# A gated mix of long convolution and attention: the convolution's tail added by GpSimd instead of TensorE, the short convolution on the whole array, 84 tiles of exponentials on VectorE

## The chip, the cores and the metric

One core of one Trainium2 chip. The metric is device time in microseconds for one execution. A core has five engines with a queue each: TensorE (PE, its weight loads are listed as PEld), VectorE (DVE), ScalarE (ACT), GpSimd (POOL) and SyncE (SP, which only issues transfers here). Each engine works its queue off in order and waits on semaphores that other engines raise.

## The reference

Sequence length S = 2048, width D = 640, 32 heads of width 20, one key and value head for all of them.

```
x = A_q;  g = sigmoid((x * gate_w).sum(-1))
a: k_shift = sum over 4 taps of A_k shifted by t, times A_shift_k     # short convolution
   kv = k_shift * A_v
   y  = causal convolution of kv with A_ssm_k, 2048 long, per channel  # by FFT in the reference
   a  = x * (y + kv * A_ssm_D)
b: q = x wq;  k = x wk;  v = x wv
   p = softmax(q k^T * 20 ** -0.5)          # 32 heads x 2048 x 2048
   b = (p v) wo
out = g * a + (1 - g) * b
```

## The kernel before, in words

**Attention.** The work is cut into 32 steps G (a block I of 512 queries, and a group of four heads that lie on four strips of 32 partitions) of 16 key blocks j. A tile is one (G, j): four strips of 128 x 512 scores. TensorE makes scores with the array split by rows (score, L1473), ScalarE takes the exponential of three or two strips at a time out of PSUM (EXP, L1510, into ETA of 1536 columns and ETB of 1024 in turn), and TensorE multiplies by the values with the array split into four strips of columns (PVmm, L1552) into PSUM bank 6. The tiles that DVE_J lists for a step go past ScalarE: their scores are made between the others (the "dqk" groups), VectorE turns them into int16 numbers (L1536, once for each strip) and makes the exponential from the bits in four passes over 2048 columns (L1545), and TensorE multiplies each of the four results by values with other weights (vneg). DVE_J holds 83 tiles.

**Normalising.** Each step ends with a copy of bank 6 by VectorE (acc, L1630), a reciprocal, a trip through memory (rbc) and a product on GpSimd (oTn or oT, L1647).

**The convolutions.** The short one (kshift, L1813 and the lines above it) is a product with diagonal matrices: for each of 5 groups of 128 channels and 4 blocks of tokens, 16 products of 128 x 128 x 128, each issued by mm4 (L822 to L825) as four matmuls on strips of 32 columns. The long one goes by transforms in two blocks of 1024: for each group c of 128 channels and each of 4 groups fc of frequencies (20 units in all) spectra (L1858) makes the spectra X of kv and K of the convolution's weights on TensorE, mac (L1910) multiplies them on GpSimd in 14 instructions (6 products Pp, 2 sums Pp, 4 sums Y, 2 sums AB), and inverse (L1932) transforms back. The second block of outputs needs X0 K1 + X1 K0 and the part of X0 K0 that runs past the first block, its tail. In the frequency domain that tail is X0 K0 turned by a quarter with a sign that alternates with fc. The kernel before folds it into K1: in spectra 16 more products of 128 columns for each unit add the turned K0 to K1's place in PSUM (8 for the real, 8 for the imaginary part), and a third plane of ssm_kT holds the negative of the first, which VectorE makes five times (kneg, L1836).

**The order of the work.** Nothing of it is written by hand. The program builds a graph of operations and a list scheduler (Scheduler) runs through it with costs, latencies and constants at the top of the file; the order on each engine is what it finds. Scores, exponentials and value products have an order of their own; everything else fills in by priority. SLACK0 says by how much a filling matmul may delay the next main one, MODE which way of splitting the array a group uses (a change of it costs SWITCH), PATIENCE, EAGER, HURRY1 and HURRY2 when VectorE's scores go in by themselves, IDLE, WAITP and HOLD when GpSimd may start beside VectorE. spectra is paced: unit u waits for the exponential at a share of 0.12 to 0.85 of them all (L1865, and the lines on soft), so the 20 units are spread evenly. If TensorE has had little to do, the scheduler puts in matmuls with zeros (L2033).

Of the kernel before, what the change touches and what calls it, by code (L numbers as in the profile page):

```python
# [7 lines left out]
ALU = mybir.AluOpType  # L8
AX = mybir.AxisListType

BF16 = dt.bfloat16
# [14 lines left out]
SLA = 0.4  # L26
SLB = 0.3
SLACK = 0.05
SLACK0 = 0.3
FILL = 0.6  # L30
FWIN = 3.4
FGAP = 0.1

MODE = {"qk": "r", "dqk": "r", "pv": "c", "fillc": "c", "q2": "m", "kc": "c", "spec": "c", "inv": "c", "op": "c", "op1": "c",
        "qpc": "c"}
SWITCH = 0.096
PATIENCE = 2.0
ROOM = 0.3
OLD = 1.0
YOUNG = 6.0  # L40
WAITN = 0.5
EAGER = 99.0
AHEAD = -1.0
HOLD = 0.05
EVP = 0.0
NPRO = 400
IDLE = 0.6
WAITP = 4.0
PVB = 2
NET = 3  # L50
NE = 5
# [133 lines left out]
class Scheduler:  # L185
# [425 lines left out]
    def emit(self, nc):  # L611
# [66 lines left out]
        for cm in reversed(cms):  # L678
# [6 lines left out]
NF = 8  # L685
NG = 4
CW = 128
# [8 lines left out]

SIDE = (7, 5)
DBK = (5, 7)
HUNGER = -5.0
PORTP = 0.05  # L700
PORTD = 0.14
PORTW = 0.1
# [11 lines left out]
REJOIN = 18  # L714
TABV = (2.2e-3, 1.05e-3)
STAGES = ((0, 256, 6), (256, 128, 5), (384, 128, 6))
DVE_J = ((), (), (3, 7, 11), (3, 5, 11, 14), (2, 8, 9), (6, 12), (2, 8, 13), (6, 9, 12),
# [4 lines left out]
SCALE = float(DH) ** -0.5  # L722
CK = SCALE * LOG2E * 128.0
OCT = math.log(2.0) / 128.0
# [38 lines left out]
C4X = 0.63  # L763
# [6 lines left out]
def c_mm(n):  # L770
    return 0.005 + 0.417e-3 * n


class Kernel:
# [67 lines left out]
    def alloc(self):  # L842
        nc = self.nc
        T = self.T
# [64 lines left out]
        spec = []  # L909
# [1 line left out]
            spec += [(f"X{i}", [128, 2, 2, 2, CW], BF16), (f"K{i}", [128, 2, 2, 2, CW], BF16)]  # L911
        spec += [("Pp", [128, 3, 2, 2, CW], F32), ("Y", [128, 2, 2, 2, CW], F32)]
        spec += [(f"EX{i}", [128, 512], F32) for i in range(NEX)]
        spec += [("ssm_kT", [128, 3, NF, CW], BF16)]
        last = [("wo", [128, NDC, D], BF16), ("oTp0", [128, NDC, 512], BF16), ("oTp1", [128, NDC, 512], BF16)]
        region("R2", early0, early, spec + late, last)
        def over(name, under, off, shape, dtype):
# [862 lines left out]
    def kshift(self):  # L1780


        T = self.T
        k, v = self.aps["A_k"][0], self.aps["A_v"][0].rearrange("(b p r) d -> p b r d", p=128, r=4)
        self.dma(T["wtap"][:, :, :], self.aps["A_shift_k"].rearrange("(c p) j -> p c j", p=128), writes=["wtap"],
                 nbytes=5120, prio=3, after=self.crow0, lat=3.0)
        self.dve(lambda e: e.memset(T["kTr"][:, :, 12:16], 0.0), (), [("kTr", -1)], 0.2, prio=20, after=self.crow0)
        w = self.g.writer
        early = [w["qT0", 1, 4]]
        for b in range(NB):  # L1790
            late = self.crow0 + (early if b > 2 else [])
            o, i = T["kTr"][:, :, 16 + 512 * b:528 + 512 * b], k[512 * b:512 * b + 512, :]
            x = self.g.add("sp", lambda e, o=o, i=i: e.dma_start_transpose(o, i), (), [("kTr", b)], 0.1, kind="d",
                           nbytes=655360, prio=14 + b, lat=1.6, after=late, name="ld_k")
            x.iss = 3.3
            self.dma(T["kv"][:, 4 * b:4 * b + 4, :], v[:, b, :, :], writes=[("kvl", b)], nbytes=655360,
                     prio=14.5 + b, name="ld_v", after=late)
        sh = [128, NDC * 4, 128]
        self.dve(lambda e: e.tensor_tensor(
            T["kdiag"][:, :, :, :].rearrange("p c j d -> p (c j) d"), T["ident"][:, :].unsqueeze(1).to_broadcast(sh),  # L1800
            T["wtap"][:, :, :].rearrange("p c j -> p (c j)").unsqueeze(2).to_broadcast(sh), ALU.mult),
            ["ident", "wtap"], ["kdiag"], c_ps(2560), prio=16, port=True, name="ksh", after=[self.g.writer["kT4", NB - 1, 0], self.wq_cp])
        for c in range(NDC):
            for q in range(NB):
                pr = 24.0 + 4.0 * c + 0.5 * q
                gr = self.group("kc", pr)
                for ii in range(4):
                    for j in range(4):
                        t0 = 16 + 512 * q + ii - j
                        self.mm(gr, lambda e, bk, ii=ii, j=j, t0=t0, c=c: self.mm4(e, self.bank(bk, 128, 128 * ii), T["kTr"][:, c, t0:t0 + 509:4], T["kdiag"][:, c, j, :],  # L1810
                            start=(j == 0), stop=(j == 3)), [("kTr", q), ("kTr", q - 1), "kdiag"], c_mm(128))
                kvp = T["kv"][:, 4 * q:4 * q + 4, 128 * c:128 * c + 128]
                self.evac(gr, "dve", lambda e, bk, kvp=kvp: e.tensor_tensor(  # L1813
                    kvp, self.bank(bk).rearrange("p (i d) -> p i d", i=4), kvp, ALU.mult), [("kvl", q)],
                    [("kv", c, 4 * q + x) for x in range(4)], c_dve(512))
# [13 lines left out]
    def ssm_kT(self, c, base):  # L1829

        T = self.T
        for blk in range(2):
            src = self.scr_k[c][1024 * blk:1024 * blk + 1024].rearrange("(b p r) d -> p b (r d)", p=128, r=4)
            self.dma(T["ssm_kT"][:, blk, :, :].rearrange("p (b r) d -> p b (r d)", r=4), src, reads=[("scr_k", c)],
                     writes=[("ssm_kT", blk)], nbytes=262144, prio=base - 100, name="ld_ssmk")
        self.dve(lambda e: e.tensor_scalar(T["ssm_kT"][:, 2, :, :], T["ssm_kT"][:, 0, :, :], -1.0, None, ALU.mult), [("ssm_kT", 0)],  # L1836
                 [("ssm_kT", 2)], C4X, port=True, prio=base - 100, name="kneg")

    def conv(self):
        T = self.T  # L1840
# [17 lines left out]
    def spectra(self, c, fc, base):  # L1858

        T = self.T  # L1860
# [2 lines left out]
        kt = T["ssm_kT"]  # L1863
        f0 = 128 * fc
        pace = self.exps[int(len(self.exps) * (PACE0 + (PACE1 - PACE0) * u / (NG * D // CW)))]  # L1865
        first = 2 if fc % 2 else 0
        for kind in ("X", "K"):
            Z, z = T[f"{kind}{p}"], (kind, p)
            ex = self.nex % NEX
# [6 lines left out]
            for par in range(2):  # L1876
# [6 lines left out]
                for comp, mc in order:  # L1883
                    n = 2 * mc + par
                    lhs, tk = self.table("TO" if par else "TE", comp, mc, f0)
                    rhs, rk = rhs_of(n)
                    if kind == "K" and (comp, mc) == (0, NG - 1):
                        if par == 0:
                            l0, t0 = self.table("TE", 0, 0, f0)
                            self.mm(gr, lambda e, bk, l0=l0: self.mm4(e, self.bank(bk, 128, 0), l0, T["Drow"][:, c % 2, :], start=False, stop=False),  # L1890
                                [t0, ("Drow", c % 2)], c_mm(128))
                        for cf in range(2):
                            pl = first if cf else 2 - first
                            for mf in range(NG):
                                l1, t1 = self.table("TO" if par else "TE", cf, mf, f0)
                                self.mm(gr, lambda e, bk, l1=l1, cf=cf, pl=pl, n=2 * mf + par: self.mm4(e, self.bank(bk, 128, 128 + 256 * (1 - cf)), l1, kt[:, pl, n, :], start=False, stop=False),
                                    [t1, ("ssm_kT", pl)], c_mm(128))
                    self.mm(gr, lambda e, bk, lhs=lhs, rhs=rhs, comp=comp, st=(comp, mc) == (0, 0), sp=(comp, mc) == (1, NG - 1): self.mm4(e, self.bank(bk, 256, 256 * comp), lhs, rhs, start=st, stop=sp), [tk] + rk, c_mm(256))
                gr.mms[0].soft = {pace} - gr.mms[0].deps
                gr.mms[0].deps |= gr.mms[0].soft  # L1900
# [9 lines left out]
    def mac(self, c, fc, p, prio):  # L1910

        T = self.T
        P, Y, W, z = T["Pp"], T["Y"], T["AB"], u_of(c, fc)

        def tt(out, a, b, alu, reads, writes, n, cost=None):
            f = lambda e: e.tensor_tensor(out, a, b, alu)  # L1916
            self.pool(f, reads, writes, cost or c_pool(n), prio=prio, port=True, name="mac")

        sh = [128, 2, 2, CW]
        for h in range(2):  # L1920
            X, K = T[f"X{p}"][:, h], T[f"K{p}"][:, h]
# [171 lines left out]
```

## Time and profile before

| | us |
|---|---|
| median of 3 runs | 820.15 (818.24 to 820.39) |
| the profiled execution's own time | 812.48 |
| its span from first to last instruction | 810.7 |

| engine | busy, us | share of the span | instructions |
|---|---|---|---|
| PE | 770.7 | 95% | 13513 |
| PEld | 317.9 | 39% | 13517 |
| DVE | 663.1 | 82% | 1102 |
| ACT | 790.6 | 98% | 706 |
| POOL | 380.4 | 47% | 370 |

The profile is of one execution. Busy time counts the stretches in which at least one instruction of an engine runs; instructions overlap, so the mean of one times the count can be more than the busy time. TensorE's four strips run side by side, and the ends of its matmuls are modelled.

### The profile page before, as it was taken

How to read it: one execution, taken by the hardware profiler on the slowest of the kernel's cores; microseconds unless marked ns; L12 is line 12 of the kernel's file. 1: busy time of each engine (PE TensorE's matmuls, PEld its weight loads, DVE VectorE, ACT ScalarE, POOL GpSimd, SP SyncE). 2: the span in 40 equal slices, each digit the busy share in tenths (PEclk: the TensorE clock that was granted, in tenths of full speed). 3: DMA queues.
4: the chain of work that ended last, by engine and by line, in shares of the span. 5: the costliest groups of instructions: out<-in, count | busy, mean ns of one | idle time of the engine just before them, and what ended most of it. 6: DMA issues, size and time to landing. Idle time of an engine off the chain costs nothing.

```text
span 810.7 us, 29855 instructions
## 1 busy us (share of the span) xinstructions
PE 770.7 (95%) x13513; PEld 317.9 (39%) x13517; DVE 663.1 (82%) x1102; ACT 790.6 (98%) x706; POOL 380.4 (47%) x370
## 2 busy tenths in 40 slices
PE   8999999999999999999999999999999999999997
PEld 5244432344323443433433433443333433243344
DVE  7757899898888788899788888888899977947954
ACT  7999999999999899999999999999999999999996
POOL 4340000058766636577445677467666664600000
PEclk9999999999999999999999999999999999999999
DMA  8889111200112000011002120001000000041111
GB/s 229 196 172 194 35 49 47 57 10 23 48 49 54 23 10 21 24 48 42 16 23 56 46 65 23 16 23 36 21 23 23 17 15 15 4 120 64 56 57 35
DMA packets 65743, 42.26 MB, mean 52 GB/s; under 512 B 43379, under 2 KB 60496, under 8 KB 65616
## 3 DMA queue, kind: packets, MB, share of 16 engines
q1 hardware_dynamic: 65040, 40.14, 18.9%
q8 instruction: 105, 1.72, 0.9%
q10 hardware_dynamic: 576, 0.22, 0.1%
q14 instruction: 22, 0.18, 0.1%
HBM read 22.93 MB, written 11.13 MB: 42 GB/s over the span
## 4 chain that ended last, share of the span: by engine, by line
ACT 61%; PE 34%; DVE 4%; issue 1%; DMA 0%; DVEq 0%
ACT ETA L1510 37%; ACT ETB L1510 24%; PE ps L1473 12%; PE ps L824 10%; PE ps L1552 9%; DVE ES L1536 1%; PE ps L2033 1%; PE ps L1199 0%; DVE ES L1545 0%; DMA xn<-in_A_q_dram 0%; PE ps L1085 0%; PE ps L1713 0%; PE ps L1380 0%; DVE X L1905 0%; DVE EX L1902 0%
## 5 line engine op out<-in xcount | busy, mean ns | idle before, releaser
L1510 ACT ACTIVATE ETA<-ps 128x1536 bf16<-128x1536 f32 x344 | 524.4, 1525 | 8.6 <-PE ps L1473 5.3
L1510 ACT ACTIVATE ETB<-ps 128x1024 bf16<-128x1024 f32 x343 | 379.6, 1107 | 0.0
L1473 PE MATMUL ps<-qT,kT 32*128 32x512 bf16 (+2 forms) x2176 | 331.8, 371 | 27.4 <-ACT ETA L1510 13.1
L1536 DVE TENSOR_SCALAR ES<-ps 128x512 int16<-128x512 f32 x332 | 221.7, 686 | 69.9 <-PE ps L1473 66.5
L1545 DVE TENSOR_SCALAR ES<-ES 128x2048 int16<-128x2048 int16 x332 | 236.8, 768 | 4.7 <-PE ps L1552 2.5
L1473 PEld LDWEIGHTS ps<-qT,kT 32*128 32x128 bf16 x2176 | 84.5, 91 | 264.2 <-ACT ETB L1510 94.4
L1916 POOL TENSOR_TENSOR Pp<-X,K 128x512 f32<-128x512 bf16 x120 | 144.0, 1211 | 68.7 <-DVE ES L1545 37.2
L1552 PE MATMUL ps<-ETA,vaug 128*32 128x512 bf16 (+2 forms) x1106 | 134.4, 369 | 0.8 <-issue 0.8
L1552 PE MATMUL ps<-ETB,vaug 128*32 128x512 bf16 (+2 forms) x738 | 133.1, 369 | 0.0
L1552 PE MATMUL ps<-ES,vneg 128*32 128x512 bf16 x1328 | 117.6, 383 | 0.0
L1647 POOL TENSOR_TENSOR oTn<-acc,rbc 128x512 bf16<-128x512 f32 x24 | 36.3, 1513 | 123.0 <-DVE ES L1545 122.5
L1916 POOL TENSOR_TENSOR Y<-Pp 128x256 f32<-128x256 f32 x80 | 59.4, 742 | 38.1 <-DVE ES L1545 30.8
L1916 POOL TENSOR_TENSOR Pp<-Pp 128x512 f32<-128x512 f32 x40 | 51.6, 1291 | 38.3 <-DVE ES L1545 29.3
L1916 POOL TENSOR_TENSOR AB<-Y 128x512 bf16<-128x512 f32 x40 | 51.7, 1302 | 26.3 <-DVE ES L1545 22.0
L1552 PEld LDWEIGHTS ps<-ES,vneg 128*32 128x32 bf16 x1328 | 33.4, 95 | 40.6 <-issue 18.6
L1647 POOL TENSOR_TENSOR oT<-acc,rbc 128x512 bf16<-128x512 f32 x7 | 10.1, 1437 | 74.9 <-DVE ES L1545 50.3
L1552 PEld LDWEIGHTS ps<-ETA,vaug 128*32 128x32 bf16 x1106 | 29.6, 94 | 31.9 <-issue 28.2
L824 PE MATMUL ps<-ssm_kT,TE 128*32 128x128 bf16 (+1 forms) x1280 | 40.1, 247 | 0.1
L824 PE MATMUL ps<-ssm_kT,TO 128*32 128x128 bf16 (+1 forms) x1280 | 38.3, 247 | 0.4 <-DVE ES L1536 0.4
L1552 PEld LDWEIGHTS ps<-ETB,vaug 128*32 128x32 bf16 x738 | 28.5, 94 | 22.3 <-issue 20.6
L2033 PE MATMUL ps<-TE,zeros 128*32 128x512 bf16 x352 | 30.7, 386 | 0.8 <-DVE acc L1630 0.8
L1905 DVE TENSOR_TENSOR K<-ps,EX 128x512 bf16<-128x512 f32 x40 | 27.2, 681 | 4.6 <-PE ps L824 4.3
(179 smaller groups left out, 673.7 us busy)
## 6 DMA issues: line engine op xcount, KB each, us to landing
rbc<-scr_d SPq DMA_DIRECT2D x31, 256.0 KB
scr_o<-oTn SPq DMA_DIRECT2D x24, 128.0 KB, 1.8
kv<-in_A_v_dram SPq DMA_DIRECT2D x4, 640.0 KB
scr_k<-kst SPq DMA_DIRECT2D x5, 512.0 KB
ssm_kT<-scr_k SPq DMA_DIRECT2D x10, 256.0 KB, 4.6
out_dram<-outsb SPq DMA_DIRECT2D x15, 160.0 KB
xn<-in_A_q_dram SPq DMA_DIRECT2D x3, 640.0 KB
scr_q<-xT SPq DMA_DIRECT2D x15, 128.0 KB, 1.7
```

Of the source, the lines that this page charges most:

```text
L824: x = e.matmul(out[q:q + 32], lhs[:, q:q + 32], rhs, tile_position=(0, q), **k)
L1473: return e.matmul(self.bank(bk, n, n * t), T["kT0" if first(G, jt) else "kT4"][32 * r:32 * r + 32, 128 * jt:128 * jt + 128], T[k][32 * r:3 ...
L1510: x = op("act", lambda e: e.activation(et(n)[:, 0:w], self.ps[:, lo:lo + w], ACT.Exp, scale=OCT, bias=-K0 * OCT), [("ps", base[n % 2] + k) ...
L1536: self.evac(gr, "dve", lambda e, bk, c=c: e.tensor_scalar(P[:, c], self.bank(bk), FINE, FTOP, ALU.mult, ALU.add), (), [kP[r]], c_dve(512))
L1545: V(lambda e, E=E, t=t: e.tensor_scalar(E, P, 1.0 / FINE, SHIFT[t] - FTOP / FINE, ALU.mult, ALU.add), kP, [("ES", z)], C4X, port=True, nam ...
L1552: return op("pe", lambda e: e.matmul(self.bank(b, n)[32 * r:32 * r + 32, :], v[:, j, :], src, start=(j == 0 or cut and j == 4 * EARLY), st ...
L1647: self.pool(lambda e: e.tensor_tensor(out, T["acc"][:, :], T["rbc"][:, :], ALU.mult), ["acc", "rbc"], [key], 1.27, prio=p, port=True, name ...
L1905: self.evac(gr, "dve", lambda e, bk, EX=EX, Z=Z, h=h, alu=alu: e.tensor_tensor(Z[:, h].rearrange("p i a c -> p a i c"), parts(self.bank(bk ...
L1916: f = lambda e: e.tensor_tensor(out, a, b, alu)
L2033: sch.filler, *sch.filler2 = ([[lambda e, r=r, st=st, b=b, n=n: e.matmul(self.bank(b, n)[32 * r:32 * r + 32, :], self.T["zeros"][:, 0:32], ...
```

## The change

In spectra the 16 products that add the tail go, with the third plane of ssm_kT and kneg. In mac two more GpSimd instructions for each unit add the turned first block's product to the second block's. The short convolution issues each product as one matmul on the whole array. There are two buffers EX instead of one, which takes the room of the third plane. DVE_J lists 84 tiles, at other places. Ten of the scheduler's constants change, so the whole order is made anew.

```diff
-SLACK0 = 0.3
+SLACK0 = 0.8
-MODE = {..., "q2": "m", "kc": "c", "spec": "c", ...}
+MODE = {..., "q2": "m", "spec": "c", ...}
-PATIENCE = 2.0
+PATIENCE = 1.4
-YOUNG = 6.0
+YOUNG = 2.0
-EAGER = 99.0
+EAGER = 0.8
-IDLE = 0.6
-WAITP = 4.0
+IDLE = 0.3
+WAITP = 6.0
-HURRY1 = 0.3
-HURRY2 = 0.2
-NEX = 1
+HURRY1 = 99.0
+HURRY2 = 0.0
+NEX = 2
-HUNGER = -5.0
+HUNGER = 0.0
-DVE_J = ((), (), (3, 7, 11), (3, 5, 11, 14), (2, 8, 9), ...
+DVE_J = ((), (), (5, 7, 10), (3, 7, 14), (3, 6, 10), ...
...
-        spec += [("ssm_kT", [128, 3, NF, CW], BF16)]
+        spec += [("ssm_kT", [128, 2, NF, CW], BF16)]
...
-    self.mm(gr, lambda e, bk, ...: self.mm4(e, self.bank(bk, 128, 128 * ii), T["kTr"][:, c, t0:t0 + 509:4], T["kdiag"][:, c, j, :],
+    self.mm(gr, lambda e, bk, ...: e.matmul(self.bank(bk, 128, 128 * ii), T["kTr"][:, c, t0:t0 + 509:4], T["kdiag"][:, c, j, :],
...
-        self.dve(lambda e: e.tensor_scalar(T["ssm_kT"][:, 2, :, :], T["ssm_kT"][:, 0, :, :], -1.0, None, ALU.mult), ...
...
-                        for cf in range(2):
-                            pl = first if cf else 2 - first
-                            for mf in range(NG):
-                                l1, t1 = self.table("TO" if par else "TE", cf, mf, f0)
-                                self.mm(gr, ..., l1, kt[:, pl, n, :], ...
...
+        for o, alu in ((fc % 2, ALU.add), (1 - fc % 2, ALU.subtract)):
+            tt(Y[:, :, 1, o, :], Y[:, :, 1, o, :], Y[:, :, 0, 1 - o, :], alu, [("Y", 0), ("Y", 1)], [("Y", 0), ("Y", 1)], 256)
```

## Rows read from the trace of the kernel before

**Rows 1.** The page: span, busy time and share of each engine
```profile
span 810.7 us, 29855 instructions
PE 770.7 (95%) x13513; PEld 317.9 (39%) x13517; DVE 663.1 (82%) x1102; ACT 790.6 (98%) x706; POOL 380.4 (47%) x370
```

**Rows 2.** ETA's exponentials: nanoseconds min/median/max, first and last start, forms
```profile
L1510 ACT ACTIVATE ETA<-ps x344: 628/1512/1710, 15.6 to 803.3; 128x1536 bf16<-128x1536 f32 x172
```

**Rows 3.** ACT in order of time: start, length, instruction, idle before it
```profile
61.51 1.45 ACT L1510 ACTIVATE ETA<-ps 128x1536 bf16<-128x1536 f32 x1 [2.11 <-PE ps L1473]
...
69.46 1.45 ACT L1510 ACTIVATE ETA<-ps 128x1536 bf16<-128x1536 f32 x1 [0.95 <-PE ps L1473]
...
780.45 1.56 ACT L1510 ACTIVATE ETA<-ps 128x1536 bf16<-128x1536 f32 x1
...
789.39 1.66 ACT L1510 ACTIVATE ETA<-ps 128x1536 bf16<-128x1536 f32 x1
```

**Rows 4.** Who ACT waited for: us in total, times, longest
```profile
ACT ETA L1510 <- PE ps L1473: 5.3, 9, 2.1
ACT ETA L1510 <- PE ps L824: 2.3, 1, 2.3
```

**Rows 5.** The chain that ended last, from 55 to 70 us
```profile
57.86 0.91 PE ps L824 x51
58.77 1.96 issue
...
67.19 0.79 issue
```

**Rows 6.** Stretches around the short convolution: PE, PEld, DVE, ACT, POOL, clock, DMA
```profile
47.00:58.00 11.00, 11.00 (x354) 6.50 (x355) 5.58 (x10) 10.96 (x10) 6.04 (x9) 1.00 0.72 154
58.00:70.00 12.00, 8.65 (x260) 4.61 (x248) 7.76 (x11) 8.93 (x9) 1.64 (x1) 1.00 1.05 171
70.00:116.00 46.00, 44.03 (x1118) 21.24 (x1118) 38.98 (x72) 45.60 (x42) 2.25 (x2) 1.00 0.35 72
```

**Rows 7.** Groups of instructions by shape: count, busy us, mean ns, idle before
```profile
L824 PE MATMUL ps<-ssm_kT,TO 128*32 128x128 bf16 x640 | 16.7, 220 | 0.0
L824 PE MATMUL ps<-ssm_kT,TE 128*32 128x128 bf16 x640 | 14.7, 220 | 0.0
L824 PE MATMUL ps<-kdiag,kTr 128*32 128x128 bf16 x1280 | 27.3, 222 | 2.1 <-issue 2.0
L1836 DVE TENSOR_SCALAR ssm_kT<-ssm_kT 128x1024 bf16<-128x1024 bf16 x5 | 3.6, 720 | 1.4 <-DMA ssm_kT<-scr_k 1.4
L1916 POOL TENSOR_TENSOR Y<-Pp 128x256 f32<-128x256 f32 x80 | 59.4, 742 | 38.1 <-DVE ES L1545 30.8 <-DVE ES L1536 1.6 <-DVE sq L1374 0.7
```

**Rows 8.** PE in order of time: changes of split, and transposes on the whole array
```profile
30.68 0.39 PE L1473 MATMUL ps<-qT,kT 32*128 32x512 bf16 x3 [0.20 <-ACT ETA L1510]
31.00 0.39 PE L1552 MATMUL ps<-ETB,vaug 128*32 128x512 bf16 x1
...
31.23 0.38 PE L1552 MATMUL ps<-ETB,vaug 128*32 128x512 bf16 x2
...
43.81 0.62 PE L1085 MATMUL ps<-ident,TI 128*128 128x128 bf16 x8
44.37 0.60 PE L1380 MATMUL ps<-sq,IndT 128*32 128x512 bf16 x2
```

**Rows 9.** Line L1916, GpSimd's products and sums: what ended idle time before them
```profile
  DVE ES L1545: 119.3, 55
  DVE K L1905: 26.5, 8
  DVE sq L1374: 6.9, 7
  DVE ES L1536: 6.3, 20
```

**Rows 10.** L1916's last group and VectorE's L1545: min/median/max ns, first and last start
```profile
L1916 POOL TENSOR_TENSOR AB<-Y x40: 1262/1272/1715, 186.4 to 708.3; 128x512 bf16<-128x512 f32 x40
L1545 DVE TENSOR_SCALAR ES<-ES x332: 623/687/1776, 66.1 to 773.5; 128x2048 int16<-128x2048 int16 x166
```

**Rows 11.** The stretch of the long convolution: all engines, then L1545 alone
```profile
167.00:709.00 542.00, 520.95 (x8877) 208.17 (x8870) 464.32 (x718) 538.14 (x476) 341.01 (x310) 1.00 0.10 29
...
167.00:709.00 542.00, 184.66 (x256) 1.00 0.10 29
```

**Rows 12.** VectorE's exponentials: groups by shape
```profile
L1536 DVE TENSOR_SCALAR ES<-ps 128x512 int16<-128x512 f32 x332 | 221.7, 686 | 69.9 <-PE ps L1473 66.5
L1545 DVE TENSOR_SCALAR ES<-ES 128x2048 int16<-128x2048 int16 x332 | 236.8, 768 | 4.7 <-PE ps L1552 2.5
```

**Rows 13.** The output projection and the last block's: by shape, then first and last start
```profile
L824 PE MATMUL ps<-wo,oTp 128*32 128x320 bf16 x480 | 24.5, 301 | 0.4 <-issue 0.3
...
L824 PE MATMUL ps<-wo,oTp x480: 296/299/310, 727.0 to 785.9; 128*32 128x320 bf16 x160
L1686 DVE SCALAR_TENSOR_TENSOR part<-ps,omgf,kv x8: 504/550/552, 787.7 to 805.3; 128x320 f32<-128x320 f32 x8
```

More of the change, by code (lines that the diff above doesn't have):

```diff
@@ L32 @@
 FGAP = 0.1
-MODE = {"qk": "r", "dqk": "r", "pv": "c", "fillc": "c", "q2": "m", "kc": "c", "spec": "c", "inv": "c", "op": "c", "op1": "c",
+MODE = {"qk": "r", "dqk": "r", "pv": "c", "fillc": "c", "q2": "m", "spec": "c", "inv": "c", "op": "c", "op1": "c",
         "qpc": "c"}
 SWITCH = 0.096
-PATIENCE = 2.0
+PATIENCE = 1.4
 ROOM = 0.3
 OLD = 1.0
-YOUNG = 6.0
+YOUNG = 2.0
 WAITN = 0.5
-EAGER = 99.0
+EAGER = 0.8
 AHEAD = -1.0
@@ L716 @@
 STAGES = ((0, 256, 6), (256, 128, 5), (384, 128, 6))
-DVE_J = ((), (), (3, 7, 11), (3, 5, 11, 14), (2, 8, 9), (6, 12), (2, 8, 13), (6, 9, 12),
[4 rows of a table removed]
+DVE_J = ((), (), (5, 7, 10), (3, 7, 14), (3, 6, 10), (7, 8, 13), (2, 10, 12), (6, 9, 11),
[4 rows of a table added]
 SCALE = float(DH) ** -0.5
@@ L1809, in kshift @@
                         t0 = 16 + 512 * q + ii - j
-                        self.mm(gr, lambda e, bk, ii=ii, j=j, t0=t0, c=c: self.mm4(e, self.bank(bk, 128, 128 * ii), T["kTr"][:, c, t0:t0 + 509:4], T["kdiag"][:, c, j, :],
+                        self.mm(gr, lambda e, bk, ii=ii, j=j, t0=t0, c=c: e.matmul(self.bank(bk, 128, 128 * ii), T["kTr"][:, c, t0:t0 + 509:4], T["kdiag"][:, c, j, :],
                             start=(j == 0), stop=(j == 3)), [("kTr", q), ("kTr", q - 1), "kdiag"], c_mm(128))
@@ L1835, in ssm_kT @@
                      writes=[("ssm_kT", blk)], nbytes=262144, prio=base - 100, name="ld_ssmk")
-        self.dve(lambda e: e.tensor_scalar(T["ssm_kT"][:, 2, :, :], T["ssm_kT"][:, 0, :, :], -1.0, None, ALU.mult), [("ssm_kT", 0)],
-                 [("ssm_kT", 2)], C4X, port=True, prio=base - 100, name="kneg")
     def conv(self):
@@ L1865, in spectra @@
         pace = self.exps[int(len(self.exps) * (PACE0 + (PACE1 - PACE0) * u / (NG * D // CW)))]
-        first = 2 if fc % 2 else 0
         for kind in ("X", "K"):
@@ L1891, in spectra @@
                                 [t0, ("Drow", c % 2)], c_mm(128))
-                        for cf in range(2):
-                            pl = first if cf else 2 - first
-                            for mf in range(NG):
-                                l1, t1 = self.table("TO" if par else "TE", cf, mf, f0)
-                                self.mm(gr, lambda e, bk, l1=l1, cf=cf, pl=pl, n=2 * mf + par: self.mm4(e, self.bank(bk, 128, 128 + 256 * (1 - cf)), l1, kt[:, pl, n, :], start=False, stop=False),
-                                    [t1, ("ssm_kT", pl)], c_mm(128))
                     self.mm(gr, lambda e, bk, lhs=lhs, rhs=rhs, comp=comp, st=(comp, mc) == (0, 0), sp=(comp, mc) == (1, NG - 1): self.mm4(e, self.bank(bk, 256, 256 * comp), lhs, rhs, start=st, stop=sp), [tk] + rk, c_mm(256))
```

8 rows, old and new, of the table DVE_J are left out of this document.

## Prediction

> **What bounds the kernel now.** I read the page first: ACT is busy 98% of the span, PE 95%, DVE 82%, POOL 47% [rows 1]. PE's figure is a poor guide, since it runs four strips side by side and much of its work is fill. So the question is whether ACT ever stops. Its exponentials start at 15.6 us and the last starts at 803.3, 787.7 us apart, 343 pairs of ETA and ETB [rows 2]. Undisturbed, four pairs take 789.39 - 780.45 = 8.94 us, 2.235 us a pair [rows 3]. 343 x 2.235 = 766.6, so ACT's row of exponentials contains about 21 us of gaps, and 15.6 us before plus 7.4 us after it belong to start and finish, which the change doesn't touch. **The kernel can get faster in two ways only: fewer columns on ACT, or fewer gaps.** It gets slower if some other engine makes new gaps, or leaves work for after the last exponential.
>
> Of the gaps the view of waits names only the long ones: 5.3 us behind scores (L1473) and 2.3 us once behind other matmuls [rows 4]. Two of the former, 2.11 and 0.95 us, lie at 61.5 and 69.5 us [rows 3], in the short convolution. There the chain that ended last is PE itself, waiting for nothing that the profile shows: 1.96 us in the middle of the short convolution's matmuls and 0.79 us a little later [rows 5]. The table by stretches says what is special: from 58 to 70 us the DMA engines are busy all the time (1.05) and PE only 8.65 of 12 us; afterwards, with the same matmuls but DMA at 0.35, PE is busy 44.03 of 46 us [rows 6]. So the stall needs a dense run of PE instructions and full DMA engines together.
>
> **The change part by part.** All sums are against the profiled execution's own 812.48 us; the three runs shown have their median at 820.15 us, 0.9% higher, so I carry the result over by ratio.
>
> *One more tile on VectorE (84 for 83).* ACT loses 4 x 512 = 2048 columns; a pair of 2560 takes 2.235 us, so ACT saves 1.79 us. VectorE gets 4 x 0.686 + 4 x 0.768 = 5.8 us [rows 12]; it stood idle 66.5 us for scores of exactly this kind [rows 12], which covers it. Without that cover the tile's values would come late and hold up the end of a step.
>
> *The tail leaves TensorE.* 1280 matmuls in two groups, 16.7 + 14.7 = 31.4 us of PE time [rows 7]. PE is not what ends last, so this counts nothing by itself; at best it thins the gaps of below a microsecond. Gaps without those three named waits: 21.1 - 2.1 - 0.9 - 2.3 = 15.8 us. I take 0 and keep both sides: half of the 15.8 us and the 2.3 us wait gone (-9), or as much again as PE fills in elsewhere under a longer SLACK0 (+5). kneg takes 3.6 us off DVE [rows 7], off the path.
>
> *The tail comes to GpSimd.* 2 instructions in each of 20 units, of the shape of Y: 40 x 0.742 = 29.7 us [rows 7], plus a wait before some of them. L1916 lost 119.3 us waiting until L1545 was done, over 280 instructions 0.43 us each [rows 9]; 40 x 0.43 = 17 us. So GpSimd needs 30 to 47 us more, in a stretch of 542 us in which it is busy 341.0 [rows 11]. I take this at nothing on the path: mac runs behind a pace set by the exponentials, and GpSimd stood waiting for its input K for 26.5 us [rows 9], nearly the bare 29.7. The other end is the first rival. AB, the last step of mac, waits for the two new sums, and inverse for AB; only the last unit's 2 x 0.74 us can't hide behind a following unit.
>
> Here a rule is to be weighed. L1545 takes 0.687 us in the median and up to 1.776 [rows 10], and it is what GpSimd waits for most [rows 9]: the two do not run together. Taken as fully exclusive, 341.0 + 184.7 = 525.7 of the 542 us are taken already [rows 11], and with 29.7 us more, 2 for the tile and 3 less of kneg it would be 554, 12 us too many. The Trainium skill, SBUF — State Buffer, section Who interferes with whom, says just this: a VectorE instruction in a two-port mode and a GpSimd instruction exclude each other for their whole length. By that rule the mac chain ends 12 us later; by the wait for K it doesn't.
>
> *The short convolution on the whole array.* 320 matmuls for 1280, and as many weight loads. On PE little changes: 27.3 us / 320 = 85 ns for four strips [rows 7], against 0.56 us / 8 = 70 ns for a whole-array product of the same size [rows 8]; 5 us of PE time, off the path. What matters is a quarter of the instructions in the stretch with full DMA engines. I take both stalls as gone, -2.11 - 0.95 = -3.06 us; the other end is 0, since the DMA load stays and the second stall came within value products. Against it: between two value products of one split 0.23 us pass, from a score to a value product 0.32 [rows 8], so a change of split costs some 0.1 us, and the short convolution now differs from both neighbours. The stretch has about 30 pairs; two changes more in each would be 6 us of PE time, against 69 - 63.7 = 5.3 us in which PE is idle there [rows 6]. The Trainium skill, TensorEngine Tiling (Array Packing), section Key Properties, has the same rule: a change of tiling mode drains the engine. By it the gain in this stretch is used up; by the pieces I expect (most lie between scores, where the split changed already) it isn't.
>
> *The second EX buffer* lets the next spectrum's evacuation start earlier: nothing on the path.
>
> **Sum:** 812.48 - 1.79 - 3.06 = 807.6 us, a ratio of 0.994; on the median 815.2 us.
>
> **The rivals.**
> 1. *GpSimd becomes the bound and the kernel is slower.* 29.7 + 17, and 2 more for the waits behind L1374 and L1536 (13.2 us over 280 instructions, times 40) [rows 9], are 49 us, less the 26.5 us of waiting for K: the last AB, now at 708.3 [rows 10], comes 22 us later. Behind it stand inverse and the output projection, 24.5 us of PE time within the 59 us from 727.0 to 785.9, and the last block's part, whose last evacuation is at 805.3 [rows 13]: there is no room behind. Each us of delay leaves 24.5 / 59 = 0.42 us of projection for after the exponentials: 9.2 us. 807.6 + 9.2 = 816.8, on the median 824.5. It decides from the point where 0.42 us times the delay exceeds the gain of 4.9: a last AB after 720 us. For it: the sum of 526 of 542 us. Against: the 26.5 us, and POOL's 59% in the stretch. With the exclusive sum alone, 12 us late, it is 807.6 + 5 = 812.7, on the median 820.5: no change.
> 2. *The gaps are only dealt anew.* The order of all engines changes; stalls of 2 to 3 us such as those at 61.5 us come up elsewhere. Only the tile is left: 810.7, on the median 818.3, no change that shows. For it: one of the three named waits has nothing to do with the short convolution. The change of split (6 us more of PE, 1 of it uncovered) ends here too.
> 3. *TensorE's relief shows.* 9 us of the other gaps go as well: 798.6, on the median 806.5. For it: 31 of 771 us of PE work go. Against: long waits for PE are few [rows 4].
> 4. *The change doesn't do what it says*: TensorE's freed time goes into matmuls with zeros. That costs nothing, and leads to rival 2.
>
> **How the numbers follow.** The bound that a measurement of this kernel can tell from no change is 0.3%, 817.7 to 822.6 us. Forecast (815.2): 0.36. Rival 1: 0.26 beyond the bound and 0.06 for its mild form by the exclusive sum. Rivals 2 and 4: 0.21. Rival 3: 0.11. Faster 0.47, same 0.27, slower 0.26. Likeliest is faster, 815.2 us, its own range 811 to 818 (both stalls gone or one, gaps 3 us fewer). The range must take in rival 1 at 824.5 with 2 or 3 us for gaps, and most of the way to rival 3: 808 to 827.
>
> **What would show it.** ACT: 2048 columns fewer, so 343 ETA or one less, and no idle time of 1 us or more between 47 and 70 us; the chain there without "issue". PE: ssm_kT with 128 columns gone, kdiag 320 times at 128*128, PE's busy time lower by some 30 us or zeros in its place. POOL: 120 Y of 256 columns, the last AB before 720 us, waiting for K below 26.5 us. The prediction is wrong in its step on GpSimd if the last AB is past 720 us and output projection runs after the last exponential; in its step on the short convolution if ACT still stops there; and in its step on gaps if span less pairs x 2.235 is still 21 us or more.

## The result and the profile after

The changed kernel takes 805.12 us in the median of four runs (804.46 to 807.77); the kernel before 819.19 (817.44 to 820.39). The ratio is 0.9836, with a 95% interval of 0.9805 to 0.9867. It is faster, then, by 1.6%, in the direction that was forecast, but by 14 us instead of 5, and below the lower end of the range.

The executions of before need a second look. The profiled one took 812.48 us, with a mean granted clock of 1.000. In the experiments' comparisons before ran some fifty times more, and no such execution came up: they lie between 816.0 and 822.9 us, with mean clocks of 0.998 to 0.987; the medians of the three sets are 819.18, 819.25 and 819.31. Those of after: 804.46 and 805.32 us at 1.000, 804.93 at 0.999, 807.77 at 0.996. The profile of before, on which every term of the sum rests, was thus its most favourable execution.

The page of after, the lines that answer to [rows 1], then the row on instruction loading and that on matmuls with zeros:

```profile
span 803.5 us, 26040 instructions
PE 759.6 (95%) x11573; PEld 304.5 (38%) x11577; DVE 663.9 (83%) x1105; ACT 788.8 (98%) x704; POOL 402.8 (50%) x410
q8 instruction: 90, 1.47, 0.8%
L2026 PE MATMUL ps<-TE,zeros 128*32 128x512 bf16 (+1 forms) x640 | 54.4, 384 | 0.4 <-DVE acc L1630 0.2
```

TensorE lost 31.4 us of tail, but its busy time fell by 11 us only. The last row shows why: matmuls with zeros take 54.4 us, where before's page has 30.7 for 352 of them. The scheduler gave 24 us of the freed time to zeros.

ACT in after: the row that answers to [rows 2], and the view of waits beside [rows 4]:

```profile
L1510 ACT ACTIVATE ETA<-ps x343: 1125/1509/1716, 15.7 to 796.7; 128x1536 bf16<-128x1536 f32 x171, 128x1024 bf16<-128x1024 f32 x1
```

```profile
ACT ETA L1510 <- PE ps L1473: 3.2, 10, 0.9
```

From the first to the last exponential 781.0 us pass; 342 pairs of 2.235 us make 764.4, which leaves 16.6 us of gaps, where before had 21.1. So the span fell by 7.2 us: 4.5 in gaps, 2.2 for one pair less (1.8 for the 2048 columns, the rest the odd piece at the end, which the tile makes longer), 0.6 in the finish, 0.1 at the start the other way. The wait of 2.3 us behind L824 is gone, and no wait of the exponentials is over 0.9 us. That accounts for the two profiles, 812.48 against 805.32. The medians differ by 14, and the other 7 us aren't in the profile of before at all.

The table by stretches [rows 6], in after; each line has the stretch and its length in us, the busy time and number of instructions of PE, PEld, DVE, ACT and POOL, the granted clock, the DMA share and GB/s:

```profile
47.00:58.00 11.00, 11.00 (x146) 6.72 (x144) 5.55 (x10) 11.00 (x10) 6.08 (x9) 1.00 0.65 144
58.00:70.00 12.00, 11.44 (x132) 5.50 (x129) 10.40 (x17) 12.00 (x12) 1.27 (x1) 1.00 1.04 175
```

From 58 to 70 us ACT works all 12 us (before 8.93), with the DMA engines as full as they were and half the PE instructions (132 for 260). The chain that ended last has no "issue" of PE there any more [rows 5]; in this stretch it goes along SP's queue:

```profile
54.97 5.16 SPq L1822
...
60.86 6.58 DMA kst<-in_A_ssm_k_dram
...
78.27 4.14 DMA den<-acc
...
82.44 0.25 DVE rcp L1640
...
85.39 1.44 ACT ETA L1510
```

A transfer for a reciprocal lands late behind the transposing loads, and ends in the one wait of 0.9 us, the longest that is left.

GpSimd: the long convolution's first product in before, then in after, then after's new sums and last group, and what its line waited for [rows 9, 10]:

```profile
L1916 POOL TENSOR_TENSOR Pp<-X,K x120: 1143/1155/1663, 167.5 to 700.4; 128x512 f32<-128x512 bf16 x120
...
L1907 POOL TENSOR_TENSOR Pp<-X,K x120: 1148/1155/1609, 152.5 to 697.9; 128x512 f32<-128x512 bf16 x120
...
L1907 POOL TENSOR_TENSOR Y<-Y x40: 723/728/736, 175.9 to 708.0; 128x256 f32<-128x256 f32 x40
L1907 POOL TENSOR_TENSOR AB<-Y x40: 1263/1272/1713, 180.0 to 713.8; 128x512 bf16<-128x512 f32 x40
...
  DVE ES L1545: 137.4, 71
  DVE K L1896: 23.1, 6
```

The sums cost 29.1 us, and the last AB starts at 713.8 us, 5.5 later than before. The first product starts at 152.5 us; before it was 167.5. The new plan gives GpSimd 15 us more room in front.

### The profile page after: what moved, and what is told of

It reads as the page before. It is cut to its first block, busy times and chain, and to the rows that moved or that the text cites. A ratio compares the mean times of both kernels' runs of the same rounds, so it can differ in the third digit from the quotient of the medians.

```text
span 803.5 us, 26040 instructions
## 1 busy us (share of the span) xinstructions
PE 759.6 (95%) x11573; PEld 304.5 (38%) x11577; DVE 663.9 (83%) x1105; ACT 788.8 (98%) x704; POOL 402.8 (50%) x410
## 4 chain that ended last, share of the span: by engine, by line
ACT 70%; PE 23%; DVE 2%; DMA 2%; SPq 2%; issue 1%
ACT ETA L1510 43%; ACT ETB L1510 28%; PE ps L1473 8%; PE ps L1552 6%; PE ps L824 5%; PE ps L2026 1%; DMA kst<-in_A_ssm_k_dram 1%; SPq L1822 1%; SPq L800 1%; DVE ES L1536 1%; PE ps L1810 1%; DMA den<-acc 1%; PE ps L1199 0%; DMA xn<-in_A_q_dram 0%; PE ps L1085 0%
## 5 line engine op out<-in xcount | busy, mean ns | idle before, releaser
L1510 ACT ACTIVATE ETA<-ps 128x1536 bf16<-128x1536 f32 (+1 forms) x343 | 521.8, 1521 | 4.3 <-PE ps L1473 3.2
L1473 PE MATMUL ps<-qT,kT 32*128 32x512 bf16 (+2 forms) x2176 | 321.0, 371 | 33.5 <-ACT ETA L1510 14.6
L1536 DVE TENSOR_SCALAR ES<-ps 128x512 int16<-128x512 f32 x336 | 222.4, 685 | 52.3 <-PE ps L1473 48.9
L1545 DVE TENSOR_SCALAR ES<-ES 128x2048 int16<-128x2048 int16 x336 | 237.9, 762 | 9.1 <-PE ps L1552 6.6
L1907 POOL TENSOR_TENSOR Pp<-X,K 128x512 f32<-128x512 bf16 x120 | 139.8, 1169 | 58.1 <-DVE ES L1545 29.0
L2026 PE MATMUL ps<-TE,zeros 128*32 128x512 bf16 (+1 forms) x640 | 54.4, 384 | 0.4 <-DVE acc L1630 0.2
L1907 POOL TENSOR_TENSOR Y<-Y 128x256 f32<-128x256 f32 x40 | 29.1, 729 | 33.2 <-DVE ES L1545 29.1
L1893 DVE COPY EX<-ps 128x512 f32<-128x512 f32 x40 | 27.2, 681 | 3.4 <-PE ps L824 3.2
L1896 DVE TENSOR_TENSOR X<-ps,EX 128x512 bf16<-128x512 f32 x40 | 27.4, 685 | 2.2 <-PE ps L824 1.6
```

Source lines behind the costliest of these rows:

```text
L1473: return e.matmul(self.bank(bk, n, n * t), T["kT0" if first(G, jt) else "kT4"][32 * r:32 * r + 32, 128 * jt:128 * jt + 128], T[k][32 * r:3 ...
L1510: x = op("act", lambda e: e.activation(et(n)[:, 0:w], self.ps[:, lo:lo + w], ACT.Exp, scale=OCT, bias=-K0 * OCT), [("ps", base[n % 2] + k) ...
L1536: self.evac(gr, "dve", lambda e, bk, c=c: e.tensor_scalar(P[:, c], self.bank(bk), FINE, FTOP, ALU.mult, ALU.add), (), [kP[r]], c_dve(512))
L1545: V(lambda e, E=E, t=t: e.tensor_scalar(E, P, 1.0 / FINE, SHIFT[t] - FTOP / FINE, ALU.mult, ALU.add), kP, [("ES", z)], C4X, port=True, nam ...
L1893: self.evac(gr, "dve", lambda e, bk, EX=EX: e.tensor_copy(EX[:, :], self.bank(bk)), (), [("EX", ex)], c_dve(512))
L1896: self.evac(gr, "dve", lambda e, bk, EX=EX, Z=Z, h=h, alu=alu: e.tensor_tensor(Z[:, h].rearrange("p i a c -> p a i c"), parts(self.bank(bk ...
```

## The experiments

In those marked *order kept* every engine has the planner's order, untouched; only the edit differs. The others are planned anew. Gaps are counted as in the prediction: from the first to the last exponential of ETA, less 2.235 us for each pair.

**Before again, unchanged (b_again).**

> The kernel before, unchanged, to see whether its 812.48 us profiled execution stands for its other executions (817 to 820 us). Theory A (stall with full DMA engines): its executions differ by the length of the stalls in the short convolution between 58 and 70 us; a profile near 818 us would show about 8 us there where the first showed 3. Rival: the difference is spread over the whole span, or lies in the start or the end; then the stretch 58 to 70 us shows the same 3 us.

Measured: 818.62 us (816.08 to 820.65), ratio 0.9994 [0.998, 1.0009]; the profile has a span of 817.9 us. Two pairs of rows show what the first profile lacked. The table by stretches in the first profile of before:

```profile
58.00:64.00 6.00, 3.43 (x126) 1.91 (x114) 2.23 (x4) 3.88 (x5) 0.00 (x0) 1.00 1.15 136
64.00:71.00 7.00, 6.08 (x173) 3.17 (x165) 5.91 (x9) 6.05 (x6) 1.64 (x1) 1.00 0.96 205
...
728.00:734.00 6.00, 5.91 (x112) 2.41 (x108) 2.96 (x6) 5.93 (x6) 0.00 (x0) 1.00 0.10 31
734.00:740.00 6.00, 6.00 (x97) 2.02 (x85) 3.48 (x6) 5.97 (x7) 0.00 (x0) 1.00 0.22 75
```

The same kernel, the same stretches, in this run:

```profile
58.00:64.00 6.00, 3.41 (x128) 1.98 (x116) 1.19 (x2) 3.62 (x4) 0.00 (x0) 1.00 1.35 147
64.00:71.00 7.00, 6.74 (x73) 1.84 (x77) 5.60 (x8) 5.13 (x5) 1.64 (x1) 0.52 0.86 190
...
728.00:734.00 6.00, 2.91 (x65) 1.32 (x57) 0.69 (x1) 2.91 (x4) 0.00 (x0) 0.95 0.36 99
734.00:740.00 6.00, 5.91 (x94) 2.22 (x86) 2.25 (x4) 4.66 (x5) 0.00 (x0) 0.77 0.02 4
```

From 58 to 64 us PE stands idle as long in both (3.43 and 3.41 us busy). Its long stall, though, is 1.96 us in the one and 2.24 in the other, where two of 0.23 and 0.24 us stand ahead of it; whether these make the difference isn't shown. The instruction after the stall, in before, in this run, and in a run further down with little to load (b_small_kst):

```profile
60.73 0.36 PE L824 MATMUL ps<-kdiag,kTr 128*32 128x128 bf16 x9 [1.96 <-issue]
...
61.77 0.36 PE L824 MATMUL ps<-kdiag,kTr 128*32 128x128 bf16 x9 [2.24 <-issue]
...
58.85 0.36 PE L824 MATMUL ps<-kdiag,kTr 128*32 128x128 bf16 x9 [0.47 <-issue]
```

After the stall the granted clock stays at 1.00 in the one and is 0.52 in the other: the level of 1.2 GHz, and only 73 instructions for 173. Near 730 us the same follows a transfer of wo that lands late, in order of time:

```profile
732.76 0.46 PE L824 MATMUL ps<-wo,oTp 128*32 128x320 bf16 x8 [3.09 <-DMA wo<-in_B_wo_dram]
...
733.69 1.45 ACT L1510 ACTIVATE ETA<-ps 128x1536 bf16<-128x1536 f32 x1 [3.09 <-PE ps L1473]
```

ACT's waits behind scores sum to 11.6 us, for 5.3 [rows 4].

```profile
L1510 ACT ACTIVATE ETA<-ps x344: 632/1514/1714, 15.8 to 810.5; 128x1536 bf16<-128x1536 f32 x172
```

The gaps are 28.1 us for 21.1, and these 7.0 us are nearly the whole difference of the spans, 817.9 - 810.7.

**The short convolution alone on the whole array, in before (b_kc_full, order kept).**

```diff
-    ... lambda e, bk, ...: self.mm4(e, self.bank(bk, 128, 128 * ii), T["kTr"]...
+    ... lambda e, bk, ...: e.matmul(self.bank(bk, 128, 128 * ii), T["kTr"]...
```

> The kernel before with the short convolution's products as one matmul on the whole array, issued in the same order as before on every engine (only the instruction's form is changed). Theory A: the stalls between 58 and 70 us go, ACT there is busy 12 of 12 us, and the time falls by 3 us at least and by up to 10 us if they are longer in most executions: 809 to 816 us. Rival 1 (the stall belongs to the full DMA engines alone): it stays, and the time is that of before, 819 us. Rival 2 (changes of split cost): slower by up to 3 us, 822 us.

Measured: 811.44 us (810.36 to 814.76), 0.9912 [0.9888, 0.9937]; its clock is 1.000 in three runs and 0.997 in one. One line of code gives 7.7 us, over half of the whole gain. The stretch, and ETA's exponentials:

```profile
58.00:70.00 12.00, 11.25 (x142) 5.95 (x141) 9.33 (x13) 12.00 (x12) 1.65 (x1) 1.00 0.98 208
...
L1510 ACT ACTIVATE ETA<-ps x344: 632/1518/1715, 15.8 to 801.0; 128x1536 bf16<-128x1536 f32 x172
```

ACT no longer stops there; the gaps are 18.6 us. Against before's good execution the span gains 2.2 us, where 3.06 were forecast: ACT works 12.00 of 12 us for 8.93, but from 70 to 116 us it is busy 44.51 us for 45.60 [rows 6], with short waits between 82 and 107 us (0.50 us the longest). Against before's usual executions it gains what follows the stall, too.

**The strips put back into after (a_kc_strips, order kept).** The same line, the other way.

> The changed kernel with the short convolution on four strips again, in the changed kernel's order. Theory A: stalls come back at 58 to 70 us and the time rises by 3 to 10 us from 805: 808 to 815 us. Rival 1: no change, 805 us; then the gain lies in the new order and in the tail.

Measured: 810.83 us (809.77 to 813.23), 0.9894 [0.9877, 0.991], 5.7 us more than after. The one execution with a clock of 1.000 took 809.77 us, so the low clock is only a part of what the strips cost here. In the profile the stall and the low clock are back:

```profile
58.00:70.00 12.00, 9.95 (x206) 4.81 (x207) 5.93 (x10) 7.44 (x7) 0.35 (x1) 0.65 1.01 184
```

**Before with strips, but with little to load (b_small_kst, order kept).** The transposing transfers of A_ssm_k, and the stores of their result, move a sixteenth; the spectra then work on other data. The first of the lines changed:

```diff
-e.dma_start_transpose(st[:, :, :], self.aps["A_ssm_k"][CW * c:CW * c + CW, :])
+e.dma_start_transpose(st[:, 0:1, :], self.aps["A_ssm_k"][CW * c:CW * c + CW, 0:128])
```

> The kernel before, strips and order unchanged, but the transposes that load the long convolution's weights move a sixteenth (and other data of the same size goes into the spectra: the output is not that of the reference). Theory A (dense PE instructions and full DMA engines together): with the DMA engines free the stalls at 58 to 70 us go although the four strips stay, granted clock 1.00 there, 809 to 813 us. Rival (dense instructions alone): the stalls stay, 817 to 820 us.

Measured: 814.32 us (811.3 to 818.42), 0.9945 [0.9921, 0.9969].

```profile
58.00:70.00 12.00, 10.68 (x322) 5.59 (x314) 9.16 (x13) 11.48 (x11) 1.66 (x1) 1.00 0.15 42
```

With the DMA share at 0.15 for 1.05 [rows 6], PE gets through 322 instructions in the 12 us, for 260, and the long stall shrinks from 1.96 us to 0.47. So the long stall needs both, many PE instructions and full DMA engines; taking away either ends it or leaves a quarter. The time is 5.0 us below before's, where 6 to 10 were expected: a late stall of 3.0 us, with the low clock behind it, remains near 728 us.

What PE waits for can be read from the trace: it is its own instructions. They come by a queue of transfers of their own, in before:

```profile
q8 instruction: 105, 1.72, 0.9%
```

That is 105 packets of 16 KB for the 13513 + 13517 instructions of PE and PEld, 257 a packet. In after 90 packets go with 11573 + 11577, again 257, and in b_kc_full 98 with 12557 + 12557, 256.

The stalls lie a packet apart. In b_again those at 51.96, 56.16 and 59.53 us come after 1217, 1473 and 1729 recorded instructions of PE and PEld, 256 from one to the next; those of a_kc_strips and b_small_kst among these products come at the same counts. In before, whose trace has four records fewer, they come after 1725 and, at 67.19 us, after 1981.

And each ends when a packet has landed. In the trace's list of transfers one goes from 58.52 to 59.48 us in before, and PE goes on at 60.73, 1.25 us after the landing. In b_again the packet lands at 60.29 and PE goes on 1.48 us later, in b_small_kst at 57.44 and 1.41 us; at the other such stalls, b_loads_free's with them, it is 1.30 to 1.75 us. In b_small_kst the packet sets out 1.9 us before PE stops, in before 0.25 us. So PE waits for its next instructions: the strips take four times as many for the same products, and beside full DMA engines the packets set out late.

**That late stall (b_loads_free, order kept).** The four transfers of a set (wo, oTp) no longer wait for each other's landing; their readers wait for the set.

```diff
+                for o in s:
+                    o.deps = base | lanes[o]
```

> The kernel before, strips and order kept, but the four loads of wo and the four of each oTp no longer wait for one another to land (they write different partitions; readers wait for all four). If the late wo load at about 733 us is the second part of what most executions of the kernel before lose, the gap of 3 us and the second episode of granted clock 0.5 there go, and the time falls from 819 to about 815 us, with the stalls at 58 to 70 us unchanged. Rival: the loads are not it, 819 us.

Measured: 816.91 us (815.12 to 818.46), 0.9974 [0.9957, 0.999]. The late stretch is whole again, but from 321 to 329 us the clock is now 0.79, where b_again has 1.00:

```profile
728.00:734.00 6.00, 6.00 (x130) 3.12 (x132) 1.38 (x2) 5.75 (x5) 0.00 (x0) 1.00 0.14 27
...
321.00:329.00 8.00, 7.45 (x115) 2.92 (x112) 4.96 (x7) 6.74 (x7) 4.99 (x5) 0.79 0.02 3
```

The gain is 2.3 us, where 4 were expected, and the short convolution (7.7 us) remains the larger cause.

**The tail taken from TensorE, nothing in its place (bk_no_tail: b_kc_full without the 1280 matmuls, order kept; the output lacks the tail).**

```diff
-self.mm(gr, lambda e, bk, l1=l1, ...: self.mm4(..., kt[:, pl, n, :], ...
+self.skip.add(self.mm(gr, lambda e, bk, l1=l1, ...: self.mm4(..., kt[:, pl, n, :], ...
```

> The kernel before with the short convolution on the whole array (b_kc_full, 811.4 us) and the tail's 1280 matmuls left out, in the same order on all engines: the output lacks the tail. It measures TensorE's relief alone. Prediction's step (off the path): 811 us within 2. Rival (31 us less for PE thins the gaps): 803 to 808 us.

Measured: 817.57 us (813.73 to 827.26), 0.9982 [0.995, 1.0013]; without the longest run the median is 816.87. That is 31 us of PE work less, and 5 to 6 us *slower* than b_kc_full; the clock was 0.977 to 0.994. The same three stretches in b_kc_full, then in bk_no_tail, there with ETA's exponentials:

```profile
316.00:324.00 8.00, 7.46 (x137) 3.08 (x137) 5.89 (x10) 8.00 (x9) 5.26 (x5) 1.00 0.02 3
324.00:340.00 16.00, 15.87 (x275) 6.53 (x271) 13.40 (x22) 16.00 (x16) 11.12 (x10) 1.00 0.09 28
...
356.00:362.00 6.00, 5.79 (x119) 2.53 (x118) 5.89 (x9) 6.00 (x7) 3.77 (x4) 1.00 0.07 22
```

```profile
316.00:324.00 8.00, 7.12 (x89) 1.92 (x77) 6.99 (x11) 8.00 (x8) 4.20 (x5) 0.91 0.00 0
324.00:340.00 16.00, 15.76 (x254) 6.42 (x252) 11.44 (x19) 15.05 (x15) 9.13 (x8) 0.94 0.09 28
...
356.00:362.00 6.00, 5.23 (x64) 1.77 (x64) 5.60 (x9) 6.00 (x6) 4.66 (x4) 0.84 0.02 7
...
L1512 ACT ACTIVATE ETA<-ps x344: 628/1532/1716, 18.4 to 805.5; 128x1536 bf16<-128x1536 f32 x172
```

Where the tail was, PE has fewer instructions (89 for 137 in the first stretch), the clock falls to 0.91 and 0.94, and ACT loses 0.95 of 16 us. In the third it falls again, to 0.84. But this profile, of an execution of 814.85 us, has 4.5 us more span than b_kc_full's, and 2.6 of them lie before the first exponential (18.4 us for 15.8), with a spell of low clock at 8 to 13 us (0.66), long before the tail's place, which begins at 152.8 us in b_kc_full; only 1.9 lie in the gaps (20.5 for 18.6). So the trace shows that the clock falls where the tail was, and ties some 1.9 us to it; the rest of the 5 to 6 between the medians isn't placed.

**The tail moved to GpSimd in the old order (bk_tail_moved: the same with the two sums before each AB, order kept).**

```diff
+        fns = [lambda e, o=o, alu=alu: e.tensor_tensor(Y[:, :, 1, o, :], Y[:, :, 1, o, :], Y[:, :, 0, 1 - o, :], alu) ...
```

> As bk_no_tail, with the two GpSimd sums of each unit put in ahead of AB, in the otherwise same order (whole computation). Prediction's step: the sums hide behind the pace, the time of bk_no_tail within 2 us. Rival 1 of the prediction: GpSimd falls behind, the last AB comes after 720 us instead of about 706, and the time is 3 to 9 us above bk_no_tail.

Measured: 828.73 us (823.68 to 831.2), 1.0111 [1.0071, 1.015], 11 us over bk_no_tail. The last group of mac in this kernel:

```profile
L1918 POOL TENSOR_TENSOR AB<-Y x40: 1263/1273/1769, 188.9 to 724.4; 128x512 bf16<-128x512 f32 x40
```

In bk_no_tail that row ends at 710.0. AB comes 14 us later (22 were forecast), and 11 to 12 us are lost (9.2 forecast), but not on the first rival's path. ETA's exponentials:

```profile
L1512 ACT ACTIVATE ETA<-ps x344: 628/1504/1715, 16.9 to 818.4; 128x1536 bf16<-128x1536 f32 x172
```

The span is 825.8 us, so 7.4 us follow the start of the last exponential, as without the sums (813.0 - 805.5 = 7.5), and no matmul of the output projection stands behind it. The loss is in the gaps, 34.9 us for 20.5: ACT waits 12.6 us behind scores for 5.3, and two spells of low clock lie between 200 and 400 us.

**After without the sums (a_no_sums, order kept; the output lacks the tail).**

```diff
-            tt(Y[:, :, 1, o, :], Y[:, :, 1, o, :], Y[:, :, 0, 1 - o, :], alu, ...
+            self.skip.add(tt(Y[:, :, 1, o, :], Y[:, :, 1, o, :], Y[:, :, 0, 1 - o, :], alu, ...
```

> The changed kernel without its 40 GpSimd sums, in its order (the output lacks the tail). If they hide, 805 us within 2; if they cost on the path, 3 to 9 us less, 796 to 802 us.

Measured: 805.09 us (804.89 to 807.67), 0.9827 [0.98, 0.9854]. In the new order the sums cost nothing that can be measured.

**After without the matmuls with zeros (a_no_zeros, order kept).**

```diff
+        self.skip = {o for o in sch.linear if o.name == "fillc"}
```

> The changed kernel without its 640 matmuls with zeros, in its order (the whole computation stays). If these zeros hold TensorE's clock, which the tail's matmuls held before, episodes of granted clock 0.5 appear in the long convolution and the time rises to 815 to 825 us. If they do not matter, 805 us within 2.

Measured: 834.21 us (830.03 to 840.95), 1.0196 [1.0134, 1.0257], with clocks of 0.928 to 0.942. The 54 us of useless work are worth 29 us, more than the 10 to 20 expected. From the page and the table by stretches:

```profile
PEclk9999999979999999997999899999879998669999
...
730.00:740.00 10.00, 7.11 (x62) 1.63 (x62) 8.23 (x15) 8.92 (x9) 3.46 (x5) 0.78 0.09 27
740.00:750.00 10.00, 9.94 (x72) 2.09 (x72) 6.98 (x11) 8.16 (x8) 4.47 (x4) 0.50 0.05 16
```

PE was busy 7.11 of 10 us; in the next 10 it is busy all along, at 1.2 GHz, for hardly more instructions.

**The tail back on TensorE in after, planned anew with one EX buffer (a_tail_pe).** The sums go; the 16 products and kneg return, as in the lines the change removed.

> The changed kernel with the tail on TensorE again (third plane, kneg, one EX buffer), its constants, its table of 84 tiles and its short convolution kept; the order is made anew. If TensorE's relief makes part of the gain, 805 plus 3 to 6 us: 808 to 811 us, and shorter if GpSimd's 40 instructions had cost anything. If the tail's place counts nothing, 805 us within 2.

Measured: 827.58 us (823.08 to 831.23), 1.01 [1.0053, 1.0147]. Slower than both. A wait of 6.0 us, behind value products, stands out in ACT's view of waits:

```profile
ACT ETB L1510 <- PE ps L1552: 6.0, 1, 6.0
```

This doesn't price the tail's place, since the order differs from 118 us on. That constants and table fit one set of operations only would agree with it; no run shows it.

**One tile back on ACT (a_83, planned anew).**

```diff
-          (10,), (2, 9, 12), ())
+          (), (2, 9, 12), ())
```

> The changed kernel with one tile fewer on VectorE (step 29 gives its only one back to ScalarE); the order up to that step is the same, behind it new. The prediction's 1.79 us for a tile: 807 us. If the tile costs VectorE or TensorE as much as it saves ScalarE: 805 us.

Measured: 817.95 us (815.56 to 823.53), 0.9989 [0.9969, 1.001]: 12.8 us more, where the columns are worth 1.8. My assumption that the order ahead of that step would stay was wrong: VectorE's and GpSimd's orders differ from some 380 us on. spectra is paced by shares of all exponentials, so another count can reach back; that this is the reason is argued, not shown. A new hole, from 580 us on:

```profile
580.00:592.00 12.00, 9.84 (x151) 3.58 (x150) 11.34 (x18) 7.35 (x8) 7.92 (x8) 1.00 0.02 3
```

**An attempt at a better version (a_better, order kept).** This goes for the wait at 85 us. Free transfers as in b_loads_free, and that reciprocal three places later:

```diff
+        r = [o for o in v if o.name == "rcp"][1]
+        to = v[v.index(r) + 3]
+        v.remove(r)
+        v.insert(v.index(to) + 1, r)
```

> The changed kernel with two edits in its order: the same loads set free, and the reciprocal that VectorE waits 4.4 us for at 82 us put three places later in its queue. The gap of 1.6 us on ACT at 82 to 85 us should become 0.5 or less; the loads were in time already: 805.1 less 1 to 1.5, about 804 us. If another wait takes its place, 805 us.

Measured: 807.22 us (804.11 to 807.9), 0.9851 [0.9819, 0.9882], not better. The wait at 85 us is gone, and a spell of low clock has come in behind it:

```profile
80.00:96.00 16.00, 15.60 (x186) 6.27 (x185) 11.75 (x23) 15.49 (x15) 1.28 (x1) 1.00 0.20 54
96.00:106.00 10.00, 9.53 (x75) 4.58 (x75) 7.64 (x15) 7.87 (x8) 0.00 (x0) 0.66 0.02 3
```

PE was busy 15.60 of 16 us ahead of it, so no stall like that at 59 us set it off; what did isn't shown. The one run at 1.000 took 804.11 us, those at 0.995 and 0.996 807.2 to 807.9. The fastest version found is the changed kernel itself.

## Why the prediction was right or wrong

**The step that failed first: "I carry the result over by ratio."** The sum gave 807.6 us against 812.48, and after's profiled execution has 805.32: off by 2.3 us. Put on the median it became 815.2, off by 10.1. I treated the 7.7 us between profile and median as noise that scales. They are a cost with a place in the kernel: after the long stall of PE the granted clock may fall to 1.2 GHz (b_again: 0.52 from 64 to 71 us), and ACT then waits for scores, 28.1 us of gaps for 21.1. The first profile is the only recorded execution of before with a clock of 1.000. The change takes the stall away, and with it what followed: b_kc_full alone moves the median by 7.7 us and the best span by 2.2. Of the 14.1 us between the medians that leaves 6.3; the spans of b_kc_full and after differ by 5.0, of which 2.2 are the pair less, 2.0 gaps and 0.7 the finish, and the last 1.3 are in no profile. The profile's 1.000, beside a time 0.9% below the median of the runs, was the hint; I noted the second and didn't ask about the first.

**Short convolution, -3.06.** The mechanism held: quarter the instructions and ACT works through the stretch (12.00 of 12 us), and b_small_kst shows that full DMA engines are the other half of it. The prediction left open what PE waits for there: it is its instructions. The size was read from one execution: 2.2 us of span there, 7.7 in the median. The change of split, weighed as 6 us of PE time against it, didn't use the gain up; the short waits from 82 to 107 us in b_kc_full may be its price or not. The rule of the Trainium skill, TensorEngine Tiling (Array Packing), section Key Properties, that changing the mode drains the engine, has no price here that a row shows by itself. The 320 products take 25.1 us (27.3 as strips; 22 forecast):

```profile
L1810 PE MATMUL ps<-kdiag,kTr 128*128 128x128 bf16 x320 | 25.1, 222 | 0.2 <-DVE ES L1536 0.2
```

**The tile, -1.79.** One pair less in after; right as far as the sum goes. a_83 couldn't test it alone.

**The tail leaving TensorE, 0 (from -9 to +5).** The second error, of about 2 us: gaps fell by 2.0 us from b_kc_full to after. The wait of 2.3 us behind L824, which I had listed and left as it was, is gone. The finish, which I had called untouched, lost 0.7. Which of constants, table and freed PE does this stays open, since each re-planned variant changed the order widely. And "this counts nothing by itself" was wrong in sign for the work alone: bk_no_tail lost 5 to 6 us, of which its trace places 1.9 behind the missing work. The fourth rival saw that the time would go into zeros, and that they cost nothing; it didn't see that without them the kernel takes 834 us.

**The sums on GpSimd, 0.** Right: a_no_sums differs by less than 1 us (805.09 and 805.12), and the last AB at 713.8 us is before the bound of 720. The reason was only half mine. The wait for K gave 3.4 of the 29.1 us (23.1 for 26.5); the larger part is the start 15 us earlier. In the old order the sums do cost: AB at 724.4 us, past 720, and 11 to 12 us lost. That this is near the first rival's 9.2 is luck: it reckoned with projection left over behind the last exponential, and there was none; the loss lay in gaps. The exclusive sum, by the rule of the Trainium skill (SBUF — State Buffer, section Who interferes with whom), can't be read off recorded durations. Between 145 and 716 us after has 368.76 us of GpSimd and 202.49 of L1545, together 571.25 of 571 us:

```profile
145.00:716.00 571.00, 540.33 (x8261) 204.48 (x8261) 496.94 (x766) 568.47 (x501) 368.76 (x352) 1.00 0.10 28
...
145.00:716.00 571.00, 202.49 (x280) 1.00 0.10 28
```

By the starts and ends of the records both run in 48.9 of these us and neither in 48.6, so the stretch is not full. The same in before, from 167 to 709 us: both in 48.5, neither in 64.9, where the prediction took all but 16 us as taken. Whether the overlap is work or a wait inside an instruction isn't shown. GpSimd's 137.4 us of waiting for L1545 agree with this rule of the Trainium skill; as a sum of recorded times it failed.

Three figures of the working were off, none of which the forecast rests on: POOL's share of the stretch from 167 to 709 us is 63% (341.0 of 542), not 59%; on the median 812.7 gives 820.4 and 798.6 gives 806.1.

## What to carry to other kernels

Before a sum is put on a median, ask whether the profiled execution is a usual one: hold its time and granted clock against several others, and where they differ, look for the stall that sets off the low clock, since a change that removes the stall removes that too. TensorE's work has a second use where another engine sets the pace: taking it away can cost more than it frees, so count what will keep the clock up afterwards. Where many small matmuls run beside full DMA engines, count the instructions as well as the busy time, since they must be brought in by transfers, too. And a planned order is fitted to its operations: test an edit with the order kept and again planned anew, and don't read the one for the other.

## What the runs showed that was not expected

- Nearly the same stall on PE (1.96 and 2.24 us; 3.43 and 3.41 us busy of 6) is followed by full clock in one execution and by 1.2 GHz in another, of the same kernel.
- TensorE ran out of instructions: its stalls in the short convolution lie 256 instructions apart, and end 1.25 to 1.75 us after a packet of 16 KB on the queue for instructions.
- 54.4 us of matmuls with zeros are worth 29 us; 31 us less useful work, without a substitute, cost 5 to 6 (1.9 of it placed).
- A clock of 0.996 instead of 1.000 costs after about 3 us (807.77 against 804.46), close to 0.004 of its time; in a_no_zeros, at 0.928 to 0.942, about half of the missing clock shows as time (29 us; 0.065 x 834 = 54).
- Removing one stall makes spells of low clock come up elsewhere (b_loads_free at 321 us, a_better at 96). Why wo lands late in b_again, and not in before's first profile or in b_kc_full, stays open.
